# Attention with its division put off: inverse sums turned once per four heads and spread by DMA

## The chip, the core and the metric

The kernel runs on one core of a Trainium2 chip. The metric is the device time of one execution in microseconds (us). TensorE (PE) multiplies matrices and transposes, VectorE (DVE), ScalarE (ACT) and GpSimd (POOL) work element by element, SyncE (SP) issues the DMAs named here. Each engine takes its instructions in a fixed order, and semaphores order them between engines.

## The reference

```python
def _A_ref(x, wq, wk, wv, wo, beta):                # x: (1, 2048, 1024); 32 heads of 32
    q, k, v = ...                                   # each (B, H, N=4 segments, L=512, Dh=32)
    g = _sigmoid(beta).reshape(1, H, 1, 1)
    for s in range(N):
        qs, ks, vs = q[:, :, s], k[:, :, s], v[:, :, s]
        p = _softmax(einsum("bhqd,bhkd->bhqk", qs, ks) * Dh ** -0.5 + mask, axis=-1)
        a_dot = einsum("bhqk,bhkd->bhqd", p, vs)
        a_mem = einsum("bhld,bhde->bhle", phi(qs), M) / (einsum("bhld,bhd->bhl", phi(qs), z)[..., None] + 1e-6)
        outs.append(g * a_mem + (1.0 - g) * a_dot)
        M, z = M + einsum("bhld,bhle->bhde", phi(ks), vs), z + phi(ks).sum(over l)
    return concat(outs) @ wo
h = x + _A_ref(_layernorm(x), wq, wk, wv, wo, beta)
return h + mlp(_layernorm(_layernorm(h)))           # 1024 -> 3584, gelu, -> 1024
```

The softmax divides each row of exponentials by the row's sum; the result is weighed with 1 - g and added to the memory's part, weighed with g. All arithmetic is float32; for products an operand is split into a high and a low half, and three products are added.

## The kernel before, in words

Sequence positions are done in two halves of 1024, each as two segments of 512. In each half the attention loops over 8 groups `g` of 4 heads and, inside, over the two segments; one pass is a *unit* (32 in all). `dense` computes a unit's key, query and value projections (24 steps, the tiles `kps`, `qps`, `vps`) and the small products of the memory. It is interleaved with `heads` of the unit before: 4 heads, each a *slot* of 6 steps. The dictionary at line 623 and `PLAN` at line 31 say which operation stands in which step, for three heads at once: the current head (logits, exponentials), the one before (`p1`, transposes of the probabilities) and the one before that (`p2`, product with the values). The order on every engine follows from this and a scheduler.

For one head, 512 queries stand in 4 blocks of 128 rows. `qk` (L533) multiplies, and a VectorE instruction (L542) adds the mask and finds the row maximum; `soft` (L547) takes exponentials on ScalarE with their row sums into `mx[:, 4:8]`. `norm` (L552) inverts two sums at a time on VectorE (L554), and GpSimd multiplies the block by the inverse and by 1 - g of the head (L557). `ptr` (L560) transposes the blocks on TensorE (L573) in three groups (`t0`, `t1`, `t2`), ScalarE writes the high half `pth` (L575) and VectorE the low half `ptl` (`sub`, L580). `av` (L582) multiplies them with the values (L593); ScalarE puts the head's part in 32 rows of the tile `ot` (L598), VectorE adds the rest (`av_out`, L604). After the fourth head GpSimd adds the memory's part `omt` (L607), where there is one (not in the first segment), and SyncE stores `ot` to DRAM (L609); the last group is split at once into `oh` and `ol` for the output projection (L612). `ot` has one buffer.

Weights are split into high and low halves by `split` (L87), the low half on GpSimd (L92) or VectorE. `psum` has three banks with the tag "d" (`ps_dense`, L51), shared by the projections and the small products.

At the end of each half (`wo_first`, L729) the output projection of the first segment is interleaved with the last unit's heads. This is called the tail below. Its products are `pwo` (`mm3`, L114); one block of its weights goes to tiles `zh` and `zl` that are made from the pool `zt` (`zx_tile`, line 1302), the others to `wh` and `wl`. The stored outputs of the second segment are loaded back and split as well (`load_o`, L680).

Of the kernel before, what the change touches and what calls it, by code (L numbers as in the profile page):

```python
# [10 lines left out]
F32 = mybir.dt.float32  # L11
F32R = mybir.dt.float32r
AF = mybir.ActivationFunctionType
ALU = mybir.AluOpType
# [3 lines left out]
P = 128  # L18
S = 2048
D = 1024  # L20
H = 32
DH = 32
# [4 lines left out]
NG = 8  # L27
HT = 1024
NT = HT // P
RA, RH, RS, PD, PS = 1.3, 14, 0.7, 20, 3  # L30
PLAN = ('q1 S2', 'q0 n0 a0', 'q2 t0 a1', 'q3 n2 s0 o', 't1', 's1 t2')
SCALE = DH ** -0.5
EPS = 1e-5
DEN_EPS = 1e-6
# [9 lines left out]
def build(tc, x, wq, wk, wv, wo, beta, w1, b1, w2, b2, out):  # L44
    nc = tc.nc
    top = ExitStack()
    const = top.enter_context(tc.tile_pool(name="const", bufs=1))
    dram = top.enter_context(tc.tile_pool(name="dram", bufs=1, space=DRAM))
    psum = top.enter_context(tc.tile_pool(name="psum", bufs=1, space=PSUM))

    def ps_dense(name):  # L51
        return psum.tile([P, 512], F32, tag="d", name=name, bufs=3)

    ident = const.tile([P, P], F32, name="ident")
# [8 lines left out]
    gate = const.tile([P, 2, H], F32, name="gate")  # L63
# [18 lines left out]
    p1_dram = [dram.tile([P, 512], F32, name=f"p1_dram{j}") for j in range(FB // 2)]  # L82
    h_dram = [[dram.tile([S // P, P, FB // 4, P], F32, name=f"h_dram{i}{s}") for s in range(2)] for i in range(2)]

    acts = {}

    def split(pool, w, hi, lo, hi_eng="vector", lo_eng="gpsimd"):  # L87
        if hi_eng == "vector":
            nc.vector.tensor_copy(hi, w)
        else:  # L90
            nc.scalar.copy(hi, w)
        getattr(nc, lo_eng).tensor_tensor(lo, w, raw(hi), op=ALU.subtract)  # L92
# [94 lines left out]
    def hooked(gen, fn, every, count):  # L187
        for n, _ in enumerate(gen):
            if n % every == every - 1 and n // every < count:
                fn(n // every)  # L190
            yield
# [152 lines left out]
    def attention(half, first):  # L344
        ab, mask = acts["ab"], acts["mask"]
# [3 lines left out]
        def tmp(name):  # L349
            return ab.tile([P, 512], F32, tag="tmp", name=name, bufs=5)  # L350

        def tmpr(name):
            return ab.tile([P, 512], F32R, tag="tmpr", name=name, bufs=6)

# [47 lines left out]
        def dense(g, sl, ws, u):  # L402
# [3 lines left out]
            if kps is None:  # L406
                kps = ps_dense("kps")
                for c in project(ws["k"], sl, "kps", kps):
                    if c >= 2:
                        next(behind, None)  # L410
                    yield
            kh, kl = tmpr("kh"), tmpr("kl")
            nc.scalar.copy(kh, kps)
            nc.vector.tensor_tensor(kl, kps, raw(kh), op=ALU.subtract)
# [3 lines left out]
            for c in project(ws["q"], sl, "qps", qps):  # L418
# [5 lines left out]
                next(behind, None)  # L424
                yield
            qh, ql = tmpr("qh"), tmpr("ql")
            nc.scalar.copy(qh, qps)
            nc.vector.tensor_tensor(ql, qps, raw(qh), op=ALU.subtract)
# [4 lines left out]
            for c in project(ws["v"], sl, "vps", vps):  # L433
                if c == 0:
                    u["qs"] = stack(qh, ql, "qs", (0, 0, 1))
                if s > 0:
                    if c == 2:
                        pq = phi_sum(qparts, "pq")
                    if c == 4:
                        while small:  # L440
                            one_small()
                        pqh, pql = tmpr("pqh"), tmpr("pql")
                        mzh = ab.tile([P, 256], F32R, name="mzh", bufs=1)[:, 0:132]
                        mzl = ab.tile([P, 256], F32R, name="mzl", bufs=1)[:, 0:132]
                        nc.scalar.copy(pqh, pq)
                        nc.gpsimd.tensor_copy(mzh, MZ[:, g, :])
                        nc.gpsimd.tensor_tensor(mzl, MZ[:, g, :], raw(mzh), op=ALU.subtract)
                    if c == 5:
                        nc.gpsimd.tensor_tensor(pql, pq, raw(pqh), op=ALU.subtract)
                if c == 1 and s < 3:  # L450
                    pkn = ps_dense("pkn")
                    for i in range(4):
                        nc.tensor.transpose(pkn[:, i * P:(i + 1) * P], pk[:, i * P:(i + 1) * P], ident)
                    pkh, pkl = tmpr("pkh"), tmpr("pkl")
                    nc.scalar.copy(pkh, pkn)
                if c == 2 and s < 3:
                    nc.vector.tensor_tensor(pkl, pkn, raw(pkh), op=ALU.subtract)
                next(behind, None)
                yield
# [70 lines left out]
        offs = [0, 128, 384, 768]  # L530
        koff = [0, 512, 1024, 896]

        def qk(st, i):  # L533
            u, j = st["u"], st["j"]
            if "pr" not in st:
                st["pr"] = ab.tile([P, 1280], F32, name="pr", bufs=2)
                st["mx"] = ab.tile([P, 32], F32, name="mx", bufs=4)
                st["nm"] = ab.tile([P, 32], F32, name="nm", bufs=4)
            n = P * (i + 1)
            pqk = psum.tile([P, 512], F32, tag="qk", name="pqk", bufs=2)  # L540
            nc.tensor.matmul(pqk[:, :n], u["qs"][j][:, i * P:(i + 1) * P], u["ks"][j][:, 0:n], start=True, stop=True)  # L541
            nc.vector.tensor_tensor_reduce(  # L542
                out=st["pr"][:, offs[i]:offs[i] + n], in0=pqk[:, :n], in1=mask[:, 512 - n:512],
                op0=ALU.add, op1=ALU.min, scale=-SCALE, scalar=3.0e38, accum_out=st["mx"][:, i:i + 1])
            soft(st, i)

        def soft(st, i):  # L547
            pr, mx = st["pr"], st["mx"]
            pi = pr[:, offs[i]:offs[i] + P * (i + 1)]
            nc.scalar.activation(pi, pi, AF.Exp, bias=mx[:, i:i + 1], scale=-1.0, accum_out=mx[:, 4 + i:5 + i])  # L550

        def norm(st, i):  # L552
            pr, mx, nm, j, g = st["pr"], st["mx"], st["nm"], st["j"], st["u"]["g"]
            nc.vector.reciprocal(nm[:, 4 + i:6 + i], mx[:, 4 + i:6 + i])  # L554
            for k in (i, i + 1):
                pi = pr[:, offs[k]:offs[k] + P * (k + 1)]
                nc.gpsimd.tensor_scalar(pi, pi, nm[:, 4 + k:5 + k], gate[:, 1, 4 * g + j:4 * g + j + 1],  # L557
                                        op0=ALU.mult, op1=ALU.mult)

        def ptr(st, n):  # L560
            grp = ((0,), (1, 3), (2,))[n]
# [38 lines left out]
        def av_out(st):  # L600
            u, j, po = st["u"], st["j"], st["po"]
            ot = u["ot"]
            b = slice(32 * j, 32 * j + 32)
            nc.vector.tensor_tensor(ot[b, :], po[0:32, :], ot[b, :], op=ALU.add)  # L604
            if j == 3:
                if u["omt"] is not None:
                    nc.gpsimd.tensor_tensor(ot, ot, u["omt"], op=ALU.add)  # L607
                if u["g"] < NG - 1:
                    nc.sync.dma_start(o_dram[u["s"]][u["g"]], ot)  # L609
                else:  # L610
                    oh, ol = o_tiles(half, u["s"] % 2)
                    split(None, ot, oh[:, NG - 1, :], ol[:, NG - 1, :], hi_eng="scalar", lo_eng="vector")  # L612
# [3 lines left out]
        def slot(cur):  # L616
            p1, p2 = pipe

            def call(st, fn, *args):
                if st:  # L620
                    fn(st, *args)

            ops = {"q": (cur, qk), "n": (cur, norm), "N": (p1, norm), "t": (p1, ptr), "s": (p1, sub), "S": (p2, sub),
                   "a": (p2, av), "o": (p2, av_out)}
            for step in PLAN:
                for op in step.split():
                    call(ops[op[0]][0], ops[op[0]][1], *[int(c) for c in op[1:]])
                yield
            pipe[0], pipe[1] = cur, p1

        def heads(u):
            for j in range(4):
                yield from slot({"u": u, "j": j})

        def tail():
            yield from slot(None)
            yield from slot(None)
# [10 lines left out]
        for g in range(NG):  # L648
            for sl in range(2):
                u = {"g": g, "s": 2 * half + sl}  # L650
                d = dense(g, sl, ws, u)
# [6 lines left out]
                else:  # L658
                    if g == NG - 1 and sl == 1:
                        d = hooked(d, lambda k: load_o(half, 0, k, ab), 3, NG - 1)  # L660
# [14 lines left out]
    def o_tiles(half, sl):  # L675
        if ("o", half, sl) not in acts:
            acts["o", half, sl] = seg_tiles(sl, "o")
        return acts["o", half, sl]

    def load_o(half, sl, g, tp):  # L680
        oh, ol = o_tiles(half, sl)
        orr = tp.tile([P, 512], F32, tag="tmp", name="orr", bufs=5)
        nc.sync.dma_start(orr, o_dram[2 * half + sl][g])
        hi, lo = oh[:, g, :], ol[:, g, :]
        if sl == 0 and g % 2 == 0:
            nc.vector.tensor_copy(hi, orr)
        else:
            op = nc.scalar.copy(hi, orr)
            if sl == 1:
                tc.add_manual_dep(op.ins, acts["mm"].ins.name, NOSYNC, reason="program order")  # L690
        (nc.vector if g % 2 else nc.gpsimd).tensor_tensor(lo, orr, raw(hi), op=ALU.subtract)
# [613 lines left out]
    for half in range(2):  # L1305
# [5 lines left out]
        ab = acts["ab"]  # L1311
# [132 lines left out]
```

## Time and profile before

| | us |
|---|---|
| median of three runs | 2301.6 (2299.87 to 2302.35) |
| span of the profiled execution | 2296.2 |
| its own time outside the span | not listed |
| time in which GpSimd was busy | 1092.4 |

The span goes from the first to the last instruction. A table of stages gives the busy time of each engine in a stretch, with the number of instructions in brackets, then the granted TensorE clock (1.00 is full), the share of the DMA engines and GB/s. A row of groups has line, engine, operation, output <- inputs, shape and count, then busy time and mean ns of one, then the idle time of the engine just before them and what ended it. A row of a timeline has start, duration, engine, line, operation. A row of the chain has start, its share of the chain in us, engine, what. PEld is TensorE's loading of the operand that stays.

### The profile page before, as it was taken

The page shows a single profiled execution, that of the slowest core. Times are in us where ns is not written, and L with a number is a line of the kernel's source. Part 1 is how long each engine was busy: PE and PEld are TensorE (multiplying, and loading weights), DVE is VectorE, ACT ScalarE, POOL GpSimd, SP SyncE. Part 2 cuts the span into 40 slices and gives each one's busy share as a digit, 9 for nine tenths or more (in the row PEclk, how much of TensorE's full clock was granted, in tenths as well). Part 3 has the DMA queues.
Part 4 walks back from the last instruction along what each step waited for, and adds up shares of the span by engine and source line. Part 5 has one row for each costly group of instructions (what it writes and reads, how often), then busy time and mean ns, then how long its engine had stood idle before and what let it go on. Part 6 is the DMA issues. An engine that isn't in the chain of part 4 may idle for free.

```text
span 2296.2 us, 35279 instructions
## 1 busy us (share of the span) xinstructions
PE 2270.4 (99%) x11769; PEld 1890.8 (82%) x11769; DVE 1540.3 (67%) x3173; ACT 1225.0 (53%) x2549; POOL 1092.4 (48%) x1134
## 2 busy tenths in 40 slices
PE   8999999999999999999999999999999999999999
PEld 6888888878888888888888887888888888888887
DVE  6777777776655565777777777565566766577563
ACT  6777777775453445777777776363344223322221
POOL 5545555555244442555555556253445554155430
PEclk9999999999999999999999999999999999999999
DMA  6333333345465654433333344466667976476762
GB/s 190 92 85 91 93 89 85 87 120 182 139 204 172 188 165 142 113 91 86 85 87 88 87 111 140 156 211 175 176 188 263 345 243 216 159 253 221 249 234 90
DMA packets 322719, 355.36 MB, mean 155 GB/s; under 512 B 26190, under 2 KB 218730, under 8 KB 322538
## 3 DMA queue, kind: packets, MB, share of 16 engines
q1 hardware_dynamic: 259370, 316.40, 45.4%
q10 hardware_dynamic: 63168, 36.71, 5.3%
q8 instruction: 93, 1.52, 0.3%
q14 instruction: 88, 0.72, 0.1%
HBM read 226.59 MB, written 76.09 MB: 132 GB/s over the span
## 4 chain that ended last, share of the span: by engine, by line
PE 91%; ACT 3%; POOL 2%; DVE 2%; issue 1%; DMA 1%; ACTq 0%; SPq 0%; POOLq 0%; DVEq 0%
PE po L1278 22%; PE bps L882 9%; PE cps L882 7%; PE dps L882 6%; PE po L593 6%; PE ppt L573 6%; PE pqk L541 3%; PE vps L116 2%; PE vps L115 2%; PE kps L115 2%; PE kps L116 2%; PE vps L117 2%; PE kps L117 2%; PE pwo L117 2%; PE pwo L116 2%; PE pwo L115 2%
## 5 line engine op out<-in xcount | busy, mean ns | idle before, releaser
L557 POOL TENSOR_SCALAR pr<-pr,nm,gate 128x128 f32<-128x128 f32 (+3 forms) x512 | 322.6, 639 | 345.9 <-DVE nm L554 260.0
L550 ACT ACTIVATE pr<-pr,mx 128x256 f32<-128x256 f32 (+3 forms) x512 | 287.6, 562 | 161.9 <-DVE mx L542 158.2
L580 DVE TENSOR_TENSOR ptl<-ppt,pth 128x512 fp32r<-128x512 f32 (+1 forms) x384 | 227.2, 599 | 86.2 <-ACT pth L575 82.0
L542 DVE CUSTOM_DVE_ANT_0 pr<-pqk,mask 128x256 f32<-128x256 f32 (+3 forms) x512 | 243.3, 484 | 46.5 <-PE pqk L541 43.7
L573 PE MATMUL ppt<-ident,pr 128*128 128x128 f32 x1280 | 223.6, 277 | 2.1 <-POOL pr L557 1.4
L575 ACT CAST pth<-ppt 128x512 fp32r<-128x512 f32 (+1 forms) x384 | 194.2, 517 | 39.0 <-PE ppt L573 33.1
L1288 DVE TENSOR_TENSOR c<-c,po 128x512 f32<-128x512 f32 x160 | 105.4, 683 | 143.1 <-PE po L1278 135.5
L573 PEld LDWEIGHTS ppt<-ident,pr 128*128 128x128 f32 x1280 | 164.6, 140 | 32.5 <-POOL pr L557 2.6
L541 PE MATMUL pqk<-ks,qs 96*128 96x256 f32 (+3 forms) x512 | 161.3, 315 | 0.0
L92 POOL TENSOR_TENSOR wl<-wr,wh 128x1024 fp32r<-128x1024 f32 x52 | 124.5, 2393 | 70.8 <-PE pqk L541 27.6
L593 PE MATMUL po<-pth,vs 128*64 128x512 f32 (+3 forms) x512 | 155.4, 326 | 0.3 <-ACT pth L575 0.2
L593 PE MATMUL po<-ptl,vs 128*64 128x512 f32 (+3 forms) x512 | 153.9, 310 | 1.3 <-DVE ptl L580 1.2
L1278 PE MATMUL po<-w2h,zh 128*128 128x512 f32 x378 | 121.1, 390 | 0.8 <-DVE zh L1218 0.4
L1135 POOL TENSOR_TENSOR w2r<-w2r 128x512 f32<-128x512 f32 x54 | 85.4, 1593 | 72.0 <-DVE c L1288 36.9
L541 PEld LDWEIGHTS pqk<-ks,qs 96*128 96x128 f32 x512 | 96.2, 188 | 21.5
L994 POOL TENSOR_TENSOR s<-r 128x512 f32<-128x512 f32 x28 | 43.6, 1559 | 143.4 <-DVE sa L1010 87.1
L882 PE MATMUL bps<-zh,sb 128*128 128x512 f32 x336 | 111.0, 391 | 0.0
L882 PE MATMUL bps<-zh,sa 128*128 128x512 f32 x336 | 110.8, 390 | 0.0
L115 PE MATMUL vps<-yh,wh 128*128 128x512 f32 x256 | 109.4, 427 | 0.9 <-DVE MZ L497 0.9
L115 PE MATMUL kps<-yh,wh 128*128 128x512 f32 (+1 forms) x264 | 110.1, 417 | 0.0
L115 PE MATMUL qps<-yh,wh 128*128 128x512 f32 x256 | 106.8, 417 | 0.0
L1278 PE MATMUL po<-w2h,hl 128*128 128x512 f32 x322 | 103.2, 390 | 0.5 <-POOL hl L1218 0.3
(241 smaller groups left out, 6657.1 us busy)
## 6 DMA issues: line engine op xcount, KB each, us to landing
hr<-h_dram SPq DMA_DIRECT2D x112, 448.0 KB, 5.4
w2r<-in_B_w SPq DMA_DIRECT2D x122, 256.0 KB, 4.4
r<-in_B_w SPq DMA_DIRECT2D x56, 512.0 KB, 4.5
h_dram<-ht ACTq DMA_DIRECT2D x84, 256.0 KB, 3.7
ks<-kh SPq DMA_DIRECT2D x256, 64.0 KB, 2.0
qs<-qh SPq DMA_DIRECT2D x256, 64.0 KB, 2.0
wr<-in_A_wo SPq DMA_DIRECT2D x32, 512.0 KB, 4.0
wx<-in_B_w SPq DMA_DIRECT2D x56, 256.0 KB, 3.5
```

The source lines that it names most:

```text
L115: nc.tensor.matmul(ps, ah, bh, start=first, stop=False)
L116: nc.tensor.matmul(ps, ah, bl, start=False, stop=False)
L541: nc.tensor.matmul(pqk[:, :n], u["qs"][j][:, i * P:(i + 1) * P], u["ks"][j][:, 0:n], start=True, stop=True)
L542: nc.vector.tensor_tensor_reduce(out=st["pr"][:, offs[i]:offs[i] + n], in0=pqk[:, :n], in1=mask[:, 512 - n:512], op0=ALU.add, op1=ALU.min, ...
L550: nc.scalar.activation(pi, pi, AF.Exp, bias=mx[:, i:i + 1], scale=-1.0, accum_out=mx[:, 4 + i:5 + i])
L557: nc.gpsimd.tensor_scalar(pi, pi, nm[:, 4 + k:5 + k], gate[:, 1, 4 * g + j:4 * g + j + 1], op0=ALU.mult, op1=ALU.mult)
L573: nc.tensor.transpose(ppt[:, o:o + P], pr[:, offs[i] + jk * P:offs[i] + (jk + 1) * P], ident)
L575: acts["pth"] = n, nc.scalar.copy(pth[:, base:base + w], ppt[:, :w])
L580: nc.vector.tensor_tensor(o, x0, x1, op=ALU.subtract)
L593: nc.tensor.matmul(po[:, P * jk:], v, st[part][:, koff[jk]:koff[jk] + w], start=(jk, part) == (0, "pth"), stop=(jk, part) == (2, "ptl"))
L882: nc.tensor.matmul(ps, x_[:, c, :], y_[:, c, :], start=first and c == 0 and n == 0, stop=last and c == 3 and n == 2, skip_group_check=True)
L1278: nc.tensor.matmul(ps, x_[:, k], y_[k], start=opens and k == 0 and i == 0, stop=closes and k == self.KP - 1 and i == 2, skip_group_check=True)
```

## The change

The probabilities stay as exponentials. For each head the four sums are inverted at once on VectorE into a tile `rs` (128 rows by 16: four heads, four blocks). After the fourth head, GpSimd multiplies the 16 columns by 1 - g; TensorE transposes them into a tile of 16 by 128 in one of the three "d" banks; ScalarE copies it to SBUF; a DMA stores these 8 KB in DRAM and a second DMA loads them back so that each head's 512 values stand in all of its 32 rows (`w`, 128 by 512). When the four heads' outputs are in `ot`, GpSimd multiplies `ot` by `w`, ahead of the memory's part. `w` lies in a quarter of one of the two tiles that `zx_tile` gives for the tail, in turn; only the last unit of a half takes it from the pool of temporary tiles.

```diff
-PLAN = ('q1 S2', 'q0 n0 a0', 'q2 t0 a1', 'q3 n2 s0 o', 't1', 's1 t2')
+PLAN = ('q1 r S2', 'q0 a0', 'q2 t0 w a1', 'q3 s0 o', 't1', 's1 t2')
...
+    r_dram = [dram.tile([16, P], F32, name=f"r_dram{k}") for k in range(2)]
...
+        scr = [acts["zt"].tile([P, 4, 512], F32, tag=f"t{x_}3", name=f"sc{x_}") for x_ in "hl"]
...
-        def norm(st, i):
-            pr, mx, nm, j, g = st["pr"], st["mx"], st["nm"], st["j"], st["u"]["g"]
-            nc.vector.reciprocal(nm[:, 4 + i:6 + i], mx[:, 4 + i:6 + i])
-            for k in (i, i + 1):
-                pi = pr[:, offs[k]:offs[k] + P * (k + 1)]
-                nc.gpsimd.tensor_scalar(pi, pi, nm[:, 4 + k:5 + k], gate[:, 1, 4 * g + j:4 * g + j + 1],
-                                        op0=ALU.mult, op1=ALU.mult)
+        def inverse(st):
+            u, j = st["u"], st["j"]
+            if j == 0:
+                u["rs"] = ab.tile([P, P], F32, name="rs", bufs=1)
+            rs = u["rs"]
+            nc.vector.reciprocal(rs[:, 4 * j:4 * j + 4], st["mx"][:, 4:8])
+            if j == 3:
+                r4 = rs[:, 0:16].rearrange("p (h i) -> p h i", i=4)
+                nc.gpsimd.tensor_tensor(r4, r4, gate[:, 1, 4 * u["g"]:4 * u["g"] + 4].unsqueeze(2).to_broadcast([P, 4, 4]),
+                                        op=ALU.mult)
+
+        def weigh(st):
+            u, j = st["u"], st["j"]
+            if j < 3:
+                return
+            n = acts["weighed"] = 1 - acts.get("weighed", 0)
+            w = u["w"] = tmp("w") if u["g"] == NG - 1 and u["s"] % 2 else scr[n][:, 1]
+            pw = ps_dense("pw")
+            nc.tensor.transpose(pw[0:16, 0:P], u["rs"][:, 0:16], ident)
+            nc.scalar.copy(w[0:16, 0:P], pw[0:16, 0:P])
+            d = r_dram[n]
+            nc.sync.dma_start(d, w[0:16, 0:P])
+            nc.sync.dma_start(w, bass.AP(tensor=d.tensor, offset=d.offset, ap=[[512, 4], [0, DH], [1, 512]]))
...
             if j == 3:
+                nc.gpsimd.tensor_tensor(ot, ot, u["w"], op=ALU.mult)
                 if u["omt"] is not None:
...
-            ops = {"q": (cur, qk), "n": (cur, norm), "N": (p1, norm), "t": (p1, ptr), "s": (p1, sub), "S": (p2, sub),
+            ops = {"q": (cur, qk), "r": (p1, inverse), "w": (p1, weigh), "t": (p1, ptr), "s": (p1, sub), "S": (p2, sub),
```

`r` stands in the first step of the next head's slot, `w` in its third. On TensorE the order of all other instructions is the same, but for the tails, where some products of the output projection, among them the first pair that needs `zl`, stand elsewhere.

1 line of the change is left out of this document (removed).

## The prediction

> **What bounds the kernel now.** I read the page first (busy time, then the chain that ended last), then the table of stages, then the costliest groups.
>
> ```profile
> span 2296.2 us, 35279 instructions
> ...
> PE 2270.4 (99%) x11769; PEld 1890.8 (82%) x11769; DVE 1540.3 (67%) x3173; ACT 1225.0 (53%) x2549; POOL 1092.4 (48%) x1134
> ...
> PE 91%; ACT 3%; POOL 2%; DVE 2%; issue 1%; DMA 1%; ACTq 0%; SPq 0%; POOLq 0%; DVEq 0%
> ```
>
> The chain lies on TensorE for 91% of the span and on GpSimd for 2%. A share over the span hides the stage, so I cut the two attention halves out of it (us, then the busy time of each engine):
>
> ```profile
> core 0: us, PE busy (x) PEld busy (x) DVE busy (x) ACT busy (x) POOL busy (x), PEclk, DMA share, GB/s
> 60.00:475.00 415.00, 414.07 (x2521) 350.21 (x2521) 308.43 (x914) 301.04 (x765) 212.77 (x300) 1.00 0.35 88
> 475.00:532.00 57.00, 53.01 (x315) 42.85 (x314) 44.46 (x124) 42.01 (x102) 31.84 (x41) 1.00 0.44 131
> 962.00:1340.00 378.00, 378.00 (x2308) 320.24 (x2307) 287.14 (x854) 280.55 (x709) 212.09 (x281) 1.00 0.34 87
> 1340.00:1410.00 70.00, 66.32 (x388) 54.07 (x387) 54.02 (x152) 50.91 (x123) 38.54 (x47) 1.00 0.38 113
> ```
>
> In the steady part of both halves TensorE is without work for 0.9 us of 793 us. In the two tails, where the last heads run beside the first output products, it idles 57.00 - 53.01 = 4.0 and 70.00 - 66.32 = 3.7 us. So what the other engines are spared can return at most some 8 us here, and what TensorE gets in addition is paid in full. The granted clock is 1.00 in every stage and I leave it so.
>
> **The change part by part.** These are the groups that it takes away or copies the form of:
>
> ```profile
> L557 POOL TENSOR_SCALAR pr<-pr,nm,gate 128x128 f32<-128x128 f32 (+3 forms) x512 | 322.6, 639 | 345.9 <-DVE nm L554 260.0
> L573 PE MATMUL ppt<-ident,pr 128*128 128x128 f32 x1280 | 223.6, 277 | 2.1 <-POOL pr L557 1.4
> L92 POOL TENSOR_TENSOR wl<-wr,wh 128x1024 fp32r<-128x1024 f32 x52 | 124.5, 2393 | 70.8 <-PE pqk L541 27.6
> L607 POOL TENSOR_TENSOR ot<-ot,omt 128x512 f32<-128x512 f32 x24 | 30.9, 1287 | 27.4 <-DVE ot L604 27.4
> L554 DVE RECIPROCAL nm<-mx 128x2 f32<-128x2 f32 x256 | 42.0, 164 | 86.2 <-ACT pr L550 85.6
> ```
>
> *Removed from GpSimd and VectorE:* 512 scalings, 322.6 us, and 256 reciprocals, of which 128 come back: 42.0 / 2 = 21 us less. All of it lies beside a full TensorE. The transposes waited for the scalings 1.4 us in the whole run (second row). Worth on the path in the steady part: nothing.
>
> *Added on GpSimd:* 32 products of 128x512 (the form of L607, 1.29 us: 41 us) and 32 of 128x16, estimated at 0.3 us each from the nearest row (10 us):
>
> ```profile
> 489.99 0.29 POOL L501 TENSOR_SCALAR MZ<-MZ,zc 128x1 f32<-128x1 f32 x1
> ```
>
> GpSimd falls from 1092 to about 820 us.
>
> *Added on TensorE:* 32 transposes of 16 columns, one per four heads. Their price is read from the chain, where back-to-back transposes show what each one adds:
>
> ```profile
> 524.18 0.44 PE ppt L573 x4
> ...
> 526.61 0.65 PE ppt L573 x6
> ```
>
> Two more cost 0.65 - 0.44 = 0.21 us, so 0.11 each: 32 x 0.11 = **3.5 us**. The rows' own mean, 277 ns, contains the overlap with the next instruction; it is the upper end, 32 x 0.277 = 8.9 us. The lower end is half the step, 1.8 us, should the 16 columns count as less. I take 0.11, the same operation in the same place behind four others.
>
> [...]
>
> Does this transpose wait? At the end of a group of four heads, in the steady part (start, us):
>
> ```profile
> 220.24 0.68 DVE L604 TENSOR_TENSOR ot<-po,ot 32x512 f32<-32x512 f32 x1
> ...
> 220.87 0.19 ACT L550 ACTIVATION_READ_ACCUMULATOR pr<-pr,mx 128x1 f32 x1
> 221.09 0.17 DVE L554 RECIPROCAL nm<-mx 128x2 f32<-128x2 f32 x1 [0.17 <-ACT pr L550]
> 225.06 0.60 PE L573 MATMUL ppt<-ident,pr 128*128 128x128 f32 x4
> 226.97 0.58 ACT L598 COPY ot<-po 32x512 f32<-32x512 f32 x1
> ```
>
> The last sum is there at 221.06, its inverse at 221.26, the product with the gate by 221.6; the new transpose stands behind the four that begin at 225.06, at 225.5. That leaves 3.9 us, more than one weight split of 2.4 us (L92) on GpSimd. No wait. Behind it in TensorE's queue stand the products of probabilities and values, whose operands are ready. Its PSUM bank is one of three that at this place hold only the running projection and the transposed values. ScalarE's copy is estimated at 0.2 (the 128x1 row) to 0.6 us (the 32x512 copy) and goes just before that copy; ScalarE is busy 301 of 415 us. No cost.
>
> *The trip through DRAM*, by
>
> ```profile
> DMA to landing us min/median/max: 2.0/2.3/3.9
> ```
>
> (the 256 KB store of the finished outputs, the nearest row for both new DMAs): the copy ends about 227.5, the store lands at 229.8, the spread load, the same 256 KB, at 232.1 to 235. SyncE's queue stands still between the two, at most 4 us; behind it are the copies of the next key halves, whose source comes later. The row of sums is needed when the fourth head's output has been added, two slots after the second head's, which is the addition of 220.24. One slot is an eighth of the two units between these pieces of the chain, (137.17 - 75.26) / 8 = 7.74 us:
>
> ```profile
> 75.26 0.59 ACT kh L413
> ...
> 137.17 0.59 ACT kh L413
> ```
>
> So it is needed at 220.24 + 15.48 + 0.68 = 236.4, and is there. The 64 issues are SyncE's, off the path.
>
> *Moved: the outputs.* Before the output store now stands one more product, 1.29 us. The single output tile is written again by ScalarE one slot after the fourth head. Adding ends at 236.4, the product and the addition behind it at 239.0, the store lands at 241.3 (242.9 at worst); ScalarE writes at 226.97 + 2 x 7.74 = 242.4. It holds by 1.1 us at the median.
>
> *The tails.* The rows of sums live in the two tiles that the first output products use for a block of weights. So the low half of that block (zl, GpSimd, 2.4 us) can be made only after the product of the last-but-one group has read its row, and TensorE's order in the changed program puts the first product that needs it later, but not late enough. First tail, then second:
>
> ```profile
> 510.77 2.38 POOL L92 TENSOR_TENSOR zl<-wr,zh 128x1024 fp32r<-128x1024 f32 x1 [0.60 <-ACT zh L91]
> ...
> 513.21 0.50 PE L116 MATMUL pwo<-zl,oh 128*128 128x512 f32 x1
> ...
> 519.28 0.69 DVE L604 TENSOR_TENSOR ot<-po,ot 32x512 f32<-32x512 f32 x1
> ...
> 520.33 0.38 PE L573 MATMUL ppt<-ident,pr 128*128 128x128 f32 x2
> ```
> ```profile
> 1391.03 0.68 DVE L604 TENSOR_TENSOR ot<-po,ot 32x512 f32<-32x512 f32 x1
> ...
> 1391.80 1.30 POOL L607 TENSOR_TENSOR ot<-ot,omt 128x512 f32<-128x512 f32 x1 [2.02 <-DVE ot L604]
> ...
> 1392.44 0.39 PE L593 MATMUL po<-pth,vs 128*64 128x512 f32 x1
> ```
>
> First: outputs added at 519.97, weighed at 521.3, zl ready at 523.7. TensorE is at the product with zl behind the transposes of 520.33, less two moved products (0.46) and with one transpose more: 520.1. It waits 3.5 us. Second: 1391.71, 1393.1, 1395.5, against 1392.44 + 0.23 - 0.46 + 0.11 = 1392.3: 3.2 us. Together 6.7 us new. What goes in return, by TensorE's waits in the tails:
>
> ```profile
> PE ppt L573 <- POOL pr L557: 1.4, 4, 0.5
> PE po L593 <- DVE ptl L580: 1.2, 3, 0.5
> ...
> PE pom L516 <- DVE om L484: 0.8, 1, 0.8
> ...
> PE pm L395 <- POOL pql L449: 0.6, 1, 0.6
> ```
>
> The first and the last stand in line behind scalings, nearly all in the tails; the third stood behind another low half on VectorE, which is put off too; the second comes late in the tails and disappears behind the new wait. They add to 4.0 us, of which I let 3.7 go. Net **+3.0 us**, between -4 (no new wait) and +6.7 (nothing goes).
>
> **Sum:** 3.5 + 3.0 = 6.5 us on the profiled execution, 2296.2 to 2302.7. Its own time isn't listed; the median of the three runs is 2301.6, 5.4 us above the span, and I take that rest as unchanged: **2308.1 us**, 0.28% more. A measurement of this kernel can tell about 0.2%, 4.6 us, from no change.
>
> **The rivals.**
> *The tails come out even* (the chain to zl is shorter, or more of the old waits go): only the transposes are left, +3.5, 2305.1 us, anywhere from 0 to +4.6. For it: the tails' 7.7 us of idling hang on a GpSimd that loses a third of its work. Against it: zl can't start before the outputs are weighed.
> *Faster: the crowding in the tails ends.* Place: the two tails. GpSimd's and VectorE's lateness there makes TensorE wait 7.7 us; without the scalings all of it goes, and the new wait doesn't come. Price: 3.5 - 7.7 = -4.2, 2297.4 us. It decides where zl is ready before TensorE asks for it, 3.5 and 3.2 us sooner than I work out. [...]
>
> [...]
>
> [...]
> *Much slower: the single output tile comes free late.* The margin was 1.1 us at the store's median and -0.5 at its longest; from there it decides. Should the spread load, in a queue with the weight loads, come 2 us after its time, ScalarE waits some 1 us in each of 30 groups and TensorE behind it: +6.5 + up to 30, 2320 us or so.
>
> That the change doesn't do what it says can be told by GpSimd's busy time alone; the removed rows leave no doubt that it falls.
>
> **How the numbers follow.** Forecast (tails wait) 0.53, tails even 0.33, faster 0.07, output tile 0.07. Slower by over 0.2% (above 2306.2): 0.53 + 0.07 = 0.60; within: 0.33; faster: 0.07. The range runs from 2303 (half-price transposes, tails even) to 2314 (transposes at 3.5, nothing returned in the tails, 2 us for a bank or a copy in the way).
>
> **What would show it.** GpSimd's busy near 820 us; the new transposes with no wait of TensorE on them; TensorE waiting 3 us in each tail for zl; the steady part longer by 0.11 us per group of four heads; no wait of ScalarE for the output store. I would be wrong if the steady stage grew by more than 4 us, or if the tails lost their idling.

## The result, and the profile after

The changed kernel takes **2319.2 us** (median of 4 runs, 2317.6 to 2322.7) against 2301.7 before: a ratio of 1.0079, with a 95% interval of 1.0064 to 1.0093. The forecast was 2308.1 and its range ended at 2314. The sign was right, the size was a third of the truth.

The page of the profiled run (its own time 2317.6 us, its span 2315.8):

```profile
span 2315.8 us, 34768 instructions
...
PE 2276.5 (98%) x11801; PEld 1897.0 (82%) x11801; DVE 1523.8 (66%) x3045; ACT 1226.5 (53%) x2581; POOL 827.9 (36%) x686
...
PE 87%; DMA 4%; ACT 3%; DVE 3%; POOL 2%; issue 1%; SPq 0%; POOLq 0%; DVEq 0%; ACTq 0%
```

GpSimd fell from 1092 to 828 us, as forecast (820). The span grew by 19.6 us all the same, 2 us more than the medians: every run listed with its span took 1.8 us more than the span, so the profiled execution before, with a span of 2296.2, took about 2298. To see where the time went, both programs were cut at the same events: ScalarE's cast of the keys `kh` of chosen units, and the first product of the stage behind the tail. First the kernel before (steady part and tail of each half), then the changed one:

```profile
core 0: us, PE busy (x) PEld busy (x) DVE busy (x) ACT busy (x) POOL busy (x), PEclk, DMA share, GB/s
107.64:480.22 372.58, 371.79 (x2265) 314.71 (x2264) 277.71 (x821) 271.63 (x690) 194.76 (x271) 1.00 0.34 87
480.22:615.08 134.86, 130.87 (x674) 106.57 (x674) 90.55 (x184) 73.24 (x140) 63.16 (x73) 1.00 0.46 151
...
950.09:1351.92 401.83, 401.83 (x2452) 340.33 (x2451) 305.14 (x910) 298.56 (x756) 223.15 (x299) 1.00 0.34 86
1351.92:1485.80 133.88, 130.20 (x674) 106.46 (x673) 89.47 (x183) 71.87 (x138) 61.83 (x71) 1.00 0.44 146
```

```profile
108.36:480.82 372.46, 371.78 (x2278) 315.77 (x2276) 271.22 (x773) 271.68 (x702) 96.90 (x103) 1.00 0.37 96
480.82:623.60 142.78, 133.76 (x676) 108.82 (x676) 91.75 (x177) 73.57 (x142) 49.81 (x50) 0.98 0.44 146
...
958.02:1360.98 402.96, 402.96 (x2466) 341.32 (x2465) 297.88 (x858) 299.08 (x768) 115.70 (x117) 1.00 0.36 95
1360.98:1505.50 144.52, 132.46 (x677) 107.61 (x676) 89.46 (x176) 72.22 (x141) 48.49 (x48) 0.99 0.43 139
```

The steady parts differ by -0.1 and +1.1 us. The tails grew from 134.9 to 142.8 and from 133.9 to 144.5 us: 7.9 + 10.6 = 18.5 of the 19.6. Each growth has two parts. TensorE is idle for longer (the stretch less its busy time: 4.0 to 9.0 us, 3.7 to 12.1), and it is also *busy* for longer on nearly the same work (676 and 677 products for 674), by 2.9 and 2.3 us; the clock column, 0.98 and 0.99, says why. The clock was 1.00 in these stages before. The mean clock of the profiled execution is 0.998, that of the three others 0.995 to 0.996.

TensorE's main waits in the first tail and, behind the dots, in the second:

```profile
PE pwo L117 <- POOL zl L93: 4.1, 1, 4.1
PE po L611 <- DVE ptl L598: 2.1, 2, 1.3
PE pwo L117 <- POOL wl L93: 1.1, 1, 1.1
...
PE pwo L117 <- POOL zl L93: 4.7, 1, 4.7
...
PE pwo L117 <- POOL wl L93: 1.8, 1, 1.8
PE po L611 <- DVE ptl L598: 1.5, 1, 1.5
```

The timeline around the 4.1 us shows the chain that the prediction described, adding, weighing, `zl`, product:

```profile
518.09 0.68 DVE L622 TENSOR_TENSOR ot<-po,ot 32x512 f32<-32x512 f32 x1
...
518.85 1.28 POOL L624 TENSOR_TENSOR ot<-ot,scl 128x512 f32<-128x512 f32 x1 [2.05 <-DVE ot L622]
...
520.21 3.38 POOL L93 TENSOR_TENSOR zl<-wr,zh 128x1024 fp32r<-128x1024 f32 x1
...
521.30 2.83 DVE L93 TENSOR_TENSOR ol<-ot,oh 128x512 fp32r<-128x512 f32 x1
...
523.64 0.80 PE L117 MATMUL pwo<-zl,oh 128*128 128x512 f32 x1 [4.12 <-POOL zl L93]
```

`zl` took 3.38 us where it took 2.38 before, beside a VectorE whose subtraction took 2.83 (0.69 to 1.12 before the change). And then the work after the gap ran at half speed. The same five microseconds in the changed kernel and in the one before, in stretches of 5 us:

```profile
520.00:525.00 5.00, 1.36 (x4) 1.18 (x5) 3.97 (x2) 2.19 (x5) 3.51 (x2) 0.78 0.07 14
525.00:530.00 5.00, 5.00 (x19) 3.82 (x18) 2.09 (x8) 1.10 (x4) 0.00 (x0) 0.54 0.56 205
```

```profile
525.00:530.00 5.00, 5.00 (x28) 4.04 (x28) 3.93 (x9) 3.17 (x8) 1.74 (x3) 1.00 0.00 0
```

Both show TensorE busy for all 5.00 us; but it did 19 products instead of 28, and the granted clock was 0.54.

### The profile page after: what moved, and what is told of

It reads as the page before. It is cut to its first block, busy times and chain, and to the rows that moved or that the text cites. A ratio compares the mean times of both kernels' runs of the same rounds, so it can differ in the third digit from the quotient of the medians.

```text
span 2315.8 us, 34768 instructions
## 1 busy us (share of the span) xinstructions
PE 2276.5 (98%) x11801; PEld 1897.0 (82%) x11801; DVE 1523.8 (66%) x3045; ACT 1226.5 (53%) x2581; POOL 827.9 (36%) x686
## 4 chain that ended last, share of the span: by engine, by line
PE 87%; DMA 4%; ACT 3%; DVE 3%; POOL 2%; issue 1%; SPq 0%; POOLq 0%; DVEq 0%; ACTq 0%
PE po L1297 23%; PE bps L901 10%; PE cps L901 7%; PE dps L901 6%; PE po L611 6%; PE ppt L591 5%; PE pqk L543 3%; PE vps L116 2%; PE vps L117 2%; PE vps L118 2%; PE qps L116 2%; PE qps L117 2%; PE qps L118 2%; PE kps L116 2%; PE kps L117 2%; PE kps L118 2%
## 5 line engine op out<-in xcount | busy, mean ns | idle before, releaser
L117 PE MATMUL kps<-yl,wh 128*128 128x512 f32 (+1 forms) x264 | 102.6, 389 | 0.1
L118 PE MATMUL kps<-yh,wl 128*128 128x512 f32 (+1 forms) x264 | 102.3, 387 | 0.0
```

The source lines that it names most:

```text
L117: nc.tensor.matmul(ps, ah, bl, start=False, stop=False)
L118: acts["mm"] = nc.tensor.matmul(ps, al, bh, start=False, stop=last)
```

## The experiments

The theories, as the expectations name them. **A**, formed from the trace above: the wait for `zl`, with its slow clock, and an order of loads in SyncE's queue make the loss. **B**, the rival from the prediction's own terms: the transposes and the trips through DRAM as such. **C**: unnormalised data lower the clock. **D** and **E** were formed on the way: D, ScalarE stands at its cast of late outputs and holds what TensorE needs next; E, the same with the fall of the clock that a gap brings. Each ratio is to the runs of the kernel before that had been made by then (2302.2 us in the end, the median of 24).

The lengths of the tails are those between the events used above:

| kernel | us (median) | ratio, 95% interval | first tail | second tail | clock |
|---|---|---|---|---|---|
| before | 2302.2 | | 134.9 | 133.9 | 1.000 |
| changed | 2319.2 | 1.0079 (1.0064 to 1.0093) | 142.8 | 144.5 | 0.998 |
| own_tile | 2324.5 | 1.0094 (1.0080 to 1.0108) | 142.7 | 145.9 | 0.996 |
| own_tile_first | 2324.0 | 1.0089 (1.0075 to 1.0103) | 142.4 | 148.6 | 0.996 |
| own_tile_last | 2318.6 | 1.0067 (1.0053 to 1.0080) | 140.4 | 147.7 | 0.996 |
| trip_other_queues | 2321.6 | 1.0084 (1.0070 to 1.0098) | 145.1 | 146.1 | 0.996 |
| own_tile_other_queues | 2317.5 | 1.0065 (1.0052 to 1.0079) | 141.7 | 142.1 | 0.997 |
| own_tile_cast_gpsimd | 2313.6 | 1.0051 (1.0039 to 1.0063) | 136.9 | 142.4 | 0.998 |
| zl_on_vector | 2310.5 | 1.0036 (1.0022 to 1.0050) | 138.6 | 146.1 | 0.999 |
| constant_row | 2303.9 | 1.0012 (1.0003 to 1.0020) | 137.0 | 135.5 | 1.000 |
| all_three | 2308.3 | 1.0025 (1.0015 to 1.0035) | 135.3 | 138.0 | 1.000 |
| turns_on_before | 2303.7 | 1.0007 (0.9998 to 1.0016) | 134.6 | 134.3 | 1.000 |
| late_outputs_1 | 2307.7 | 1.0026 (1.0017 to 1.0035) | 137.2 | 136.4 | 1.000 |
| late_outputs_3 | 2311.4 | 1.0042 (1.0028 to 1.0056) | 140.4 | 142.5 | 0.998 |

Tails and clock are those of the one profiled run of each kernel, whose time isn't always near the median: it is 2305.1 for all_three and 2303.8 for late_outputs_1, but 2322.2 for own_tile_last, 2316.8 for late_outputs_3, 2306.4 for constant_row and 2313.3 for zl_on_vector. So a tail of the table holds for that execution. The times of the kernel before spread over 6 us (2298.8 to 2304.7), those of own_tile_other_queues, with mean clocks from 0.996 to 0.999, over 11 (2311.5 to 2322.3).

### The row in a tile of its own

```diff
-            w = u["w"] = tmp("w") if u["g"] == NG - 1 and u["s"] % 2 else scr[n][:, 1]
+            w = u["w"] = ab.tile([P, 512], F32, name="w", bufs=1)
```

Six small tiles (`mzh`, `mzl`, `rs`, `zc`, `rg`, `mx`) are narrowed to what they hold, to make room.

> The row of inverse sums gets a tile of its own (2 KB, made room for by narrowing six small tiles); nothing else of the computation changes. Theory A, from the trace of the changed kernel: two things in the two tails make the loss, (1) the low half zl of the weight block waits for the weighing of the last-but-one group, because the row lies in its tile: TensorE stands 4.1 and 4.7 us and then works for some 5 us at a clock of 0.54 to 0.7, together about 6.7 + 6.3 = 13.0 us; (2) the row of the last group takes one of the five scratch tiles, so three loads of output halves stand in SyncE's queue behind a weight load that waits 20 and 17.9 us, and later products wait: 2.9 + 4.1 = 7.0 us. Both go here: 2319.2 - 20 = 2299 us, between 2297 and 2304, the clock 1.000, no wait for zl over 1 us. Rival B: the round trip through DRAM in SyncE's queue and the 32 transposes are the loss; both stay, so 2315 or more. Rival C: unnormalised probabilities make TensorE's clock fall; it stays at 0.995 to 0.998 and the time at 2312 or more.

Measured: 2324.5, 5 us *slower* than the changed kernel, where A had 2297 to 2304. The wait for `zl` did go (0.3 and 0.8 us). In its place stood others. TensorE's longest waits in this run's two tails:

```profile
PE po L609 <- ACT pth L591: 3.5, 1, 3.5
...
PE po L609 <- DVE ptl L596: 3.2, 1, 3.2
```

And the rows behind the first of them:

```profile
523.50 1.26 POOL L622 TENSOR_TENSOR ot<-ot,w 128x512 f32<-128x512 f32 x1 [4.31 <-DMA w<-r_dram]
...
524.79 0.62 ACT L92 CAST oh<-ot 128x512 fp32r<-128x512 f32 x1 [4.46 <-POOL ot L622]
...
526.79 0.58 PE L609 MATMUL po<-pth,vs 128*64 128x384 f32 x1 [3.49 <-ACT pth L591]
```

The outputs of the last-but-one group were added by 521.2 us, but the row landed only at 523.5. ScalarE, whose next instruction was the cast of these outputs, stood 4.5 us, and the exponentials and copies of the last group stood behind it. In the kernel before, ScalarE's waits for the same cast, in the first and the second tail, were:

```profile
ACT oh L91 <- DVE ot L604: 0.9, 1, 0.9
...
ACT oh L91 <- POOL ot L607: 0.8, 1, 0.8
```

In the changed kernel it stood 2.2 and 5.4 us there, hidden behind the wait for `zl`. So A fell as it was put: there are two chains side by side, and taking one away leaves the other. This is theory D.

### One of the two rows at a time

In own_tile_first the own tile is used only where `u["g"] == NG - 1 and u["s"] % 2 == 0`, in own_tile_last only where `u["g"] == NG - 1 and u["s"] % 2`; everywhere else the row lies where the changed kernel has it.

> Only the last group of the first segment in each half has its row in a tile of its own; the last group of the second segment keeps the scratch tile. Nothing of the computation is left out. Theory A: zl's wait and the slow clock go (13.0 us), the order of loads in SyncE's queue stays (7.0 us): 2306 us, between 2303 and 2309, clock 1.000. Rival B (the trip): no change, 2317 to 2321. Rival C (clock by the data): clock below 1.000.

> The mirror of the run before: only the last group of the second segment has its row in a tile of its own instead of a scratch tile; the last-but-one group's row stays in the tile of zl. Nothing of the computation is left out. Theory A: the loads of output halves go before the third weight load again (7.0 us back), zl's wait of 4.1 and 4.7 us with its slow clock stays (13.0 us): 2312 us, between 2309 and 2316, clock 0.996 to 0.998. Rival B (the trip): 2317 to 2321. If the two losses overlap, this run and the one before add to less than the run with both.

Measured: 2324.0 and 2318.6, both above A's ranges (2303 to 2309, 2309 to 2316). The first is as slow as the own-tile run, for the same cause: little wait for `zl` (0.3 and 1.2 us), but 3.5 and 4.2 us for `pth` and `ptl`. The second tests the order of loads. In the changed kernel's SyncE queue three loads of output halves stood behind a weight load that waited for GpSimd, and then came at once:

```profile
SPq L719 <- POOL wl L93: 20.0, 1, 20.0
```

```profile
548.39 1.37 SPq L702 DMA_DIRECT2D orr<-o_dram  x3
```

With the last row out of the scratch tiles the order was as before the change, and of the first tail's waits the one for `ptl` fell from 2.1 to 0.8 us, while `zl` stayed:

```profile
PE pwo L117 <- POOL zl L93: 4.1, 1, 4.1
...
PE po L611 <- DVE ptl L598: 0.8, 1, 0.8
```

The first tail became 2.4 us shorter (expected 2.9), but only 1.3 of it is idling; the other 1.1 is busy time, since the clock was down for 3.4 us here (525.7 to 529.1) and for 6.8 in the changed kernel. The second became 3.2 longer: there the clock fell three times instead of once, besides the gap for `zl` also at 1365.3, behind a wait of 2.3 us for `kl`, and at 1478.0, behind one of 1.9 for `wl`. So the order of loads shows in the wait for `ptl`, 1.3 us in one tail; the total of 7 was not shown.

### The trip on other queues

```diff
-            nc.sync.dma_start(d, w[0:16, 0:P])
-            nc.sync.dma_start(w, bass.AP(...))
+            nc.scalar.dma_start(d, w[0:16, 0:P])
+            nc.gpsimd.dma_start(w, bass.AP(...))
```

> As the changed kernel, but the store of the turned sums is issued by ScalarE and the spread load by GpSimd, so SyncE's queue has no part of the trip; tiles and order of everything else stay. Nothing of the computation is left out. Theory A: the loss hangs on tiles, not on SyncE standing still for the trip (1.0 to 2.0 us each): 2317 to 2321 us, perhaps some us more if GpSimd, standing still for the trip, makes zl later. Rival B: the trip in SyncE's queue held the loads behind it: 2305 to 2313 us.

Measured: 2321.6, 0.6 us above A's 2317 to 2321, for which some more was allowed, and outside B's 2305 to 2313. With the wait for `zl` in place, SyncE's standing still for the trip is not the cause.

> Both edits together: the row of inverse sums in a tile of its own, and the store of the sums issued by ScalarE, the spread load by GpSimd. Nothing of the computation is left out. Theory A, as it was put, has fallen: the wait for zl went with the own tile, yet TensorE stood 3.5 and 3.2 us for operands of the probabilities. Theory D takes its place: in the tails the outputs of the last-but-one group are finished later than before, because they wait for their row (in the own-tile run the spread load was issued behind weight loads and landed 2.3 us and more after the adding), and ScalarE, which casts these outputs in line (it stood 4.5 and 4.3 us at that cast, 0.9 and 0.8 before the change), holds the exponentials and copies behind it; the gap of more than 3 us then costs another 2.6 us at half clock. By D the row is early here and there is no zl wait: ScalarE stands at that cast for at most the weighing, some 2 and 3 us, TensorE for under 1.5 us, clock 1.000, 2300 to 2308 us. Rival B (the 32 transposes and the trips as such cost the time): 2315 or more. Rival C (data and clock): clock under 0.998 and 2312 or more.

Measured: 2317.5, slower than D's 2300 to 2308, though 7 us faster than with the own tile and the trip in SyncE's queue. In its first tail the spread load was issued at 513.5 us, but the weighing began only at 521.6, 1.6 us after the adding, with VectorE long done. The trace gives the times from issue to landing of the 32 spread loads (L574) in this run:

```profile
DMA to landing us min/median/max: 4.8/5.3/8.0
```

513.5 and 8.0 make 521.5: the row was late here too. ScalarE stood 3.7 us at the cast, TensorE 2.8. The kind of loss is D's; that the row would be early on these queues was wrong. In the second tail ScalarE stood at the cast for 1.8 us only, as D had it, and yet the clock fell, at 1397.8, in two shorter waits of TensorE (1.1 and 0.8 us; see the last section): that is not in D.

### The outputs split by GpSimd, and the floor

```diff
-                    split(None, ot, oh[:, NG - 1, :], ol[:, NG - 1, :], hi_eng="scalar", lo_eng="vector")
+                    nc.gpsimd.tensor_copy(oh[:, NG - 1, :], ot)              # first segment only
+                    nc.gpsimd.tensor_tensor(ol[:, NG - 1, :], ot, raw(oh[:, NG - 1, :]), op=ALU.subtract)
```

> The own-tile kernel with SyncE's trip as it was (2324 us), only that GpSimd instead of ScalarE and VectorE splits the outputs of the last group of the first segment into upper and lower half. Nothing of the computation is left out. Theory D: the row comes as late as in the own-tile run, but nothing stands behind the cast, so the exponentials go on and TensorE doesn't stop: 2300 to 2308 us, clock 1.000, no wait for operands of the probabilities over 1.5 us. If D is wrong and it is the lateness of the outputs for the output products themselves: TensorE waits for the halves of the outputs, and 2315 or more.

Measured: 2313.6, above D's 2300 to 2308, but 11 us less than with the cast on ScalarE, with the trip in SyncE's queue as there: the first tail is 136.9 us, 5.8 shorter, and in it TensorE waits for probabilities for 1.1 us where it waited 4.3. The rest, and the clock of 0.998, sit in the second tail. There the clock falls at 1362.4, behind a wait of 1.8 us for `kl`, and at two gaps that are each shorter still:

```profile
1392.01 0.27 PE L570 MATMUL pw<-ident,rs 128*16 128x128 f32 x1 [1.64 <-DVE rg L484]
...
1394.08 0.79 PE L117 MATMUL pwo<-zl,oh 128*128 128x512 f32 x1 [1.24 <-POOL zl L93]
```

```profile
1390.00:1400.00 10.00, 7.12 (x28) 5.51 (x27) 6.52 (x19) 4.45 (x12) 3.59 (x2) 0.66 0.36 111
```

Together 2.9 us of idling within 3.7 us; the clock went down to 0.50 at 1393.1, when 1.9 of them had passed.

```diff
-            pw = ps_dense("pw")
-            nc.tensor.transpose(...); nc.scalar.copy(...); d = r_dram[n]; nc.sync.dma_start(...); nc.sync.dma_start(...)
+            u["w"] = acts["w"]      # one tile, set once
```

> The own-tile kernel without the 32 transposes, copies, stores and spread loads: all outputs are weighed with one constant row, so the division by the sums and the gate are left out of the result, while the inverse sums are still computed. It gives the floor of the scheme. Theory D: no late row; the added products on GpSimd are off the path: 2297 to 2303 us, as before the change. If the weighing on GpSimd itself makes the outputs late enough to stop TensorE in the tails: 2305 or more with waits behind the cast of 3 us.

Measured: 2303.9, 0.12% above the kernel before, and 1 us above the 2297 to 2303 expected. Without turns, trips and late rows this arrangement loses 2 us and gains nothing, though GpSimd is busy for 826.8 us instead of 1092.4: its work was hardly ever on the path. The weighing alone still holds ScalarE at the cast for 2.2 us in each tail, and TensorE 1.3 us behind it in the first.

### What a gap does to the clock

```diff
-            wts[0, k] = wo_halves(wo_raw(0, k), k, wo_home() if k < 3 else ...)
+            wts[0, k] = wo_halves(wo_raw(0, k), k % 3, wo_home() if k < 3 else ...)     # k = 3: VectorE
```

> The changed kernel, row in zl's tile and trip in SyncE's queue, only that VectorE makes that zl (1.2 us beside 3.4 on GpSimd). Nothing of the computation is left out. It shortens the gap of TensorE from 4.1 and 4.7 us to some 2 to 3 us and asks what the clock does. If the clock falls only after a gap longer than that: it stays at 1.000 and the time goes down by the shorter gaps and the saved slow clock, 2 x (2 + 2.6) = 9 us: 2308 to 2312. If any gap of this kind lets it fall, or if it falls for another reason: clock 0.996 to 0.998, 2313 to 2318.

Measured: 2310.5, the time of the first branch, but with a clock of 0.999 and not 1.000. The two tails of the profiled run part the two answers. In the first the gap was 1.6 us and the clock stayed; in the second it was 3.8 us and the clock fell to 0.50 for 6.8 us:

```profile
PE pwo L117 <- DVE zl L93: 1.6, 1, 1.6
...
PE pwo L117 <- DVE zl L93: 3.8, 1, 3.8
```

```profile
520.00:530.00 10.00, 9.56 (x52) 7.91 (x53) 8.88 (x24) 6.24 (x17) 0.00 (x0) 1.00 0.33 107
```

The window is the one behind the short gap. The first tail is 138.6 instead of 142.8 us: TensorE idles 1.8 us less (the gap itself is 2.5 shorter) and is busy 2.4 us less with as many products, which is the clock. C is out: the data are as unnormalised as in the changed kernel, and the clock is 1.00 in this tail, as it is in the changed kernel's steady parts.

### Lateness alone, transposes alone, and all edits together

```diff
+                if u["g"] == NG - 1 and u["s"] % 2 == 0:
+                    for _ in range(3):          # late_outputs_1: range(1)
+                        nc.gpsimd.tensor_tensor(ot, ot, u["w"], op=ALU.mult)
```

> The constant-row kernel (division and gate left out of the result) with one weighing more on GpSimd, 1.29 us, for the last group of the first segment of each half alone, so that its outputs come that much later at ScalarE's cast. It adds the suspected cost by itself, without transposes, trips or tiles. Theory E: in the first tail, where TensorE already stands 1.3 us for an operand of the probabilities behind that cast, the gap grows to some 2.6 us and the clock falls: 1.3 + 2.6 = 4 us; in the second ScalarE has more slack, 0 to 4 us. 2305 to 2312. If lateness at the cast is harmless: 2302 to 2305.

> As the run before with three weighings more, 3.9 us later (division and gate left out of the result). Theory E: gaps of 4 us or more in both tails and a clock of 0.996 to 0.998, 5 to 7 us in each: 2313 to 2318, about what the change itself costs. If lateness at the cast is harmless: 2302 to 2305. If only the gaps count and not the clock: 2 x 3.9 = 8 us at most, under 2312.

Measured: 2307.7 and 2311.4. The first is in its range, though in the profiled run (2303.8) the gap in the first tail was 1.9 us where 2.6 was expected, and the clock stayed; nine of its eleven runs have a mean clock of 0.999, against two of 24 of the kernel before. The second missed its 2313 to 2318 by 2 us and shows the whole mechanism added by itself, without transposes, trips or shared tiles:

```profile
524.95 0.62 ACT L92 CAST oh<-ot 128x512 fp32r<-128x512 f32 x1 [3.00 <-POOL ot L622]
...
526.68 0.33 PE L606 MATMUL po<-ptl,vs 128*64 128x256 f32 x1 [2.29 <-DVE ptl L593]
```

```profile
524.00:534.00 10.00, 7.71 (x35) 6.21 (x34) 6.84 (x20) 5.56 (x16) 0.92 (x1) 0.83 0.01 2
```

ScalarE stands 3.0 us at the cast, TensorE 2.3 us for what stands behind it, and the clock is 0.83 over the ten microseconds. Three weighings cost the tails 3.4 and 7.0 us over the constant row in the profiled runs (2316.8 and 2306.4 us); by the medians they cost 7.5 us in all.

```diff
+        def turned(st):                       # at the place of "w" in PLAN, third head step
+            if st["j"] < 3: return
+            pw = ps_dense("pw")
+            nc.tensor.transpose(pw[0:16, 0:P], ident[:, 0:16], ident)
+            nc.scalar.copy(turns[0:16, :], pw[0:16, 0:P])
```

> The kernel before, with only the 32 transposes of 16 columns and ScalarE's copy of each added at the place that they have in the changed kernel (they turn a piece of the unit matrix and nobody reads the result). Nothing of the computation is left out. By the spacing in the chain, 0.08 to 0.11 us each: 2.6 to 3.5 us more, 2304.5 to 2306, of which most can hide behind the steady part's own stalls. By each one's own 277 ns: 8.9 us, 2311. If a transposition that waits for its bank in the tails lets the clock fall, up to 5 us more.

Measured: 2303.7, a ratio of 1.0007 (0.9998 to 1.0016): 1.5 us for all 32, not clear of nothing, and both tails moved by less than half a microsecond. (Two small tiles, `mzh` and `mzl`, are narrowed for this.) The transposes are out as the cause; for the trips the run on other queues and the next one speak.

> The three edits together: the row in its own tile, the trip on the queues of ScalarE and GpSimd, and the outputs of the last group of the first segment split by GpSimd. Nothing of the computation is left out. Theory E (D with the clock): all that the change costs beyond its 32 transposes is lost in the two tails, by waits and by the clock that falls to 0.50 when TensorE has been idle for some 1.8 us or more within about 3.4 us. If the three edits remove every gap of that size: the constant-row kernel's 2304 plus 32 x 0.08 = 2.6 us, 2304 to 2309, clock 1.000. In the second tail the GpSimd-cast run still had 1.6 us (a transposition of the sums waiting for its bank) and 1.2 us (zl) one behind the other, and the clock fell: if these stay, 2309 to 2314 and a clock of 0.998. Rival B (trips and transposes as such): 2313 or more with the clock at 1.000.

Measured: 2308.3, 11 us less than the changed kernel, at the upper end of the first branch and well below B's 2313. All 32 transposes and trips are still there; with whatever else is left they cost 4.4 us over the constant row. The second tail still has the two small gaps, but shorter, and the clock holds in the profiled run. That run took 2305.1; six of the seven others have a mean clock of 0.998 or 0.999, so the falls of the clock aren't all gone:

```profile
PE pw L570 <- DVE rg L484: 1.1, 1, 1.1
PE pwo L117 <- POOL zl L93: 0.8, 1, 0.8
```

```profile
1386.00:1396.00 10.00, 8.10 (x48) 6.18 (x47) 7.81 (x22) 7.78 (x19) 4.28 (x3) 1.00 0.47 123
```

It is still 0.25% slower than the kernel before (interval 0.15 to 0.35%). No run of the scheme beat that kernel, nor did the constant row, which leaves out the turning and the trip.

## Why the prediction was wrong, step by step

*What bounds the kernel: right.* The steady parts stayed full (372.58 to 372.46 us, 401.83 to 402.96). Their growth is under the 4 us named as the test. The other test, tails that lose their idling, wasn't met either: they idle more.

*32 transposes, 3.5 us: right in kind, too high.* In the second steady part 14 of them cost 1.1 us, 0.08 each; in the first, 13 hid in stalls. Alone on the kernel before they cost 1.5 us. The upper end of 8.9 us, by the rows' own mean of 277 ns, did not show.

*The new transposition doesn't wait, and the trip is in time: right in the steady part.* (In the second tail the transposition waits 1.1 us for its bank, `PE pw L572 <- DVE rg L486`; before, the product that stood there, `pm`, had the same wait of 1.1.) In the steady part the trace has:

```profile
227.74 0.32 SPq L575 DMA_DIRECT2D r_dram<-sch  x1
229.13 0.58 SPq L576 DMA_DIRECT2D sch<-r_dram  x1
```

```profile
237.97 1.29 POOL L624 TENSOR_TENSOR ot<-ot,sch 128x512 f32<-128x512 f32 x1 [0.21 <-DVE ot L622]
...
243.09 0.58 ACT L616 COPY ot<-po 32x512 f32<-32x512 f32 x1 [0.43 <-DMA o_dram<-ot]
```

The weighing waits for the adding and not for the row. But ScalarE waited 0.4 us for the output tile where a margin of 1.1 was forecast, 5.5 us in 13 such waits, all hidden. The rival "output tile late" did not come: the list of TensorE's waits is empty in these stretches.

*The tails, +3.0: this is the step that failed.* Four terms of it, by the waits and stages above:

- *New waits for `zl`, 3.5 + 3.2:* measured 4.1 + 4.7. The place and the order of events were right; `zl` took 3.4 us instead of the 2.4 assumed, beside VectorE's own subtractions, and in the second tail it began 1 us late: the adding ended at 1400.9, but the row landed only at 1401.7 and the weighing began at 1401.8.
- *"The granted clock is 1.00 in every stage and I leave it so":* wrong, and worth most of 2.9 + 2.3 us in the changed kernel (TensorE worked for 6.0 and 3.4 us at 0.50, so 3.0 and 1.7 are the clock's). No gap of the kernel before is longer than 1.1 us in the tails, so its clock says nothing about gaps of 4.
- *3.7 us of old waits go:* the waits for scaled probabilities (1.2 us) and for `pql` and `pr` (0.6 each) went, 2.4 us. But `om` stayed (0.9 for 0.8), `ptl` came later instead of earlier (4.2 us, where `ptl` and `pth` had 1.4 before), `kl` cost 1.1 more, and a wait for `wl` of 1.1 + 1.8 us appeared.
- *The trip in the tail, and what stands behind the weighing.* The landing of 2.3 to 3.9 us, taken from the stores, was too short (4.8 to 8.0 us for the spread loads of the run with its own tile and the other queues), and the cast on ScalarE was not asked at all in the tail, where the last group's outputs are not stored but cast in line. In the changed kernel this chain is hidden by the one for `zl`; it alone, in the own-tile run, keeps the whole loss.

Put together for the changed kernel: 8.8 + 5.2 + 2.8 + 1.1 + 2.9 - 2.4 = 18.4, against 18.5 measured in the tails. The forecast's 3.5 for transposes was 2 too much and its 3.0 for the tails 15.5 too little.

*The rivals.* "Tails even" and "faster" needed a `zl` that is ready early; it was 0.6 and 1.5 us later than forecast. In the first tail GpSimd's `zl` (520.21 to 523.59) began 0.05 us behind a VectorE subtraction and took 1.0 us longer than before (3.38 us for 2.38), and the `ol` that VectorE began behind that one took 2.83 us and ended 0.5 us after `zl`. So `zl` took longer at the moment when TensorE waited for it.

*What stays open.* The wait for `wl`, 1.1 and 1.8 us, is there in every variant of the scheme (0.5 to 1.9 us, also without trips, in the constant-row run, 1.5 and 1.6); neither its cause nor that of the wait for `kl` was tried alone. Nor was the clock moved by a gap in the otherwise unchanged kernel before. And how the changed kernel's three other executions, with clocks of 0.995 and 0.996, divide between gaps and clock is not known, since only the one with 0.998 was profiled.

## What to carry to other kernels

Where an engine has slack everywhere but in a short crowded stage, work out that stage alone: what each in-order queue holds behind the instruction that the change makes later, ScalarE's as much as TensorE's. If two chains end late side by side, taking one away can show nothing; try them together before dropping either. And a gap of TensorE has two prices here, its length and the slow products behind it: at a clock of 0.50 behind gaps of 2.3, 3.8, 4.1 and 4.7 us, behind some of 1.8 and 1.9 us and not behind others. The same program may pay the second in one execution and not in the next (late_outputs_1: a mean clock of 0.999 in nine of eleven runs, of 1.000 in two).

## What the runs showed of the hardware

The clock of TensorE fell behind gaps of a few microseconds. In the changed kernel it went to 0.50 behind gaps of 4.1 and 4.7 us (from 519.5 and 1401.9), in the run with `zl` on VectorE behind one of 3.8, in the run with three weighings more behind one of 2.3. It stayed at 1.00 behind gaps of 1.66 and 1.75 us in the changed kernel (from 1786.0 and 1472.3) and of 1.6 in the run with `zl` on VectorE.

From 1.8 to 1.93 us both happened. The clock fell behind a wait of 1.8 for `kl` in own_tile_cast_gpsimd and one of 1.9 for `wl` in own_tile_last; it stayed over a gap of 1.93 us in the changed kernel, for `kl` (from 1361.7), and over one of 1.9 in late_outputs_1. So the 1.8 us of theory E is a size at which the clock fell in some places, not one at which it always did; what decides was not shown. The same two waits, 1.1 us of the transposition for its bank and 0.8 us for `zl`, also did both: in the run with its own tile and the other queues the clock fell behind them (first two rows), and in the run with all three edits it stayed (last three):

```profile
1394.43:1397.84 3.41, 1.61 (x7) 0.68 (x5) 2.92 (x10) 3.27 (x8) 3.41 (x2) 1.00 0.01 2
1397.84:1401.25 3.41, 3.30 (x13) 2.91 (x14) 1.59 (x4) 0.96 (x3) 0.75 (x2) 0.50 0.55 165
...
1385.08:1388.49 3.41, 2.32 (x15) 1.70 (x14) 2.90 (x8) 3.36 (x8) 2.52 (x2) 1.00 0.03 12
1388.49:1391.91 3.42, 2.61 (x17) 1.96 (x17) 2.44 (x7) 1.88 (x5) 1.79 (x2) 1.00 0.32 84
1391.91:1395.32 3.41, 3.41 (x24) 2.84 (x23) 2.80 (x11) 2.76 (x8) 0.00 (x0) 1.00 0.86 237
```

In the first row the idling before the fall was 1.8 us in 3.41, and not in one piece; in the third and fourth it was 1.1 and 0.8 us, and the clock stayed. Once down, the clock stayed down for 3.4 us (the second tail of the changed kernel, 1406.86 to 1410.27; the run with three weighings more, 528.2 to 531.6) or for 6.8 (the first tail of the changed kernel, 522.80 to 529.63), and TensorE did about half as many products in this time (14 in the 5 us from 524.0, 30 in those from 530.0).
